# Attention and a channel mix on one core: from 448-token tiles, with receptance inside the attention stage, to 512-token tiles, with receptance by seven products in a stage of its own

## The chip, the cores and the metric

The kernel runs on one core of a Trainium2 chip. Its engines are TensorE (PE in the profile, with its weight loads as PEld), VectorE (DVE), ScalarE (ACT), GpSimd (POOL) and SyncE (SP); here SP issues every DMA, POOL does next to nothing. The metric is the time of one execution on the device in microseconds, the median of three runs.

## The reference, cut to what matters

```python
# q, k, v: 8 batches, 12 heads, 448 tokens, head size 64, float32
scores = scale * (q @ k.T) - log(448)
attn   = sigmoid(scores) @ v
x      = attn, heads joined                      # (8, 448, 768)
x_prev = x shifted by one token, zero in front
xk = mu_k * x + (1 - mu_k) * x_prev
xr = mu_r * x + (1 - mu_r) * x_prev
k  = relu(xk @ w_k)                              # w_k: 768 x 1024, float64
v  = (k * k) @ w_v                               # w_v: 1024 x 768, float64
out = sigmoid(xr @ w_r) * v                      # w_r: 768 x 768, float64
```

The three weights arrive as float64 and are turned into float32 by bit operations on DVE. Most products are made in three passes of a reduced format (fp32r): both operands are split into a high part (a cast on ACT or DVE) and a low part (a subtraction on DVE), and high x high, high x low and low x high are summed in a PSUM bank.

## The kernel before

**Order.** `Plan` (lines 23 to 95) takes operations with an engine, an estimated cost, a priority and the keys that they read and write; it plays them through by these costs and sends them out in that order. The order on each engine in the built program is the one that counts.

**Attention** (lines 306 to 403). 96 heads make 48 head pairs n. `prepare` splits q and k of a pair; `scores` makes three chunks of 128 keys (each 3 x 2 half-height matmuls into one of three double banks `sc`), `sigmoid` (ACT) turns a chunk into `pf`; `score_tails` and a sigmoid do the last 64 keys of two pairs at once; `weigh` and `weigh_tails` multiply with v in native fp32 into the banks `av`. `gather` copies the result to `xx`, stores x to `x_d`, mixes xr and splits it into `xr`, which stays in SBUF.

**Receptance** (lines 406 to 441) is a plain product: 48 units (8 batches x 6 blocks of 128 outputs), each 6 x 3 products of 448 columns. 40 units stand inside attention, from head pair 10 (`R_FROM`) on, between the score chunks, as 36 half-height matmuls each (L416); 8 follow it (L434 to L436). The whole of w_r stays in SBUF for this.

**Channel mix** (lines 541 to 732). Two stages: 0 is xk @ w_k, 1 is k2 @ w_v. Both use Strassen's scheme in Winograd's form: a pair of batches, that is two tiles of 448 tokens, and the halves of the weight give seven products instead of eight. Each product is a step of 36 matmuls (L664) into four banks `xb` or `yb`. The seven combined weights are made during attention (`convert_seven`), stored, and loaded and split into seven `slots` by `load_weight`. `fetch` loads x from `x_d` and mixes xk on ACT and DVE (L575, L576); `minus` forms the combinations of the data, `operand` splits them (L588, L589); `evacuate` adds the products up on DVE from PSUM and the copy `p1s` (L693 to L713), and `out_block` applies relu and square, or multiplies with the receptance `r_d`. There are 4 pairs x 7 = 28 steps in each stage. The products are put in the order 0, 1, 5, 4, 6, 2, 3.

Of the kernel before, what the change touches and what calls it, by code (L numbers as in the profile page):

```python
# [98 lines left out]
def attention_then_channel_mix(  # L99
# [33 lines left out]
    NEG_LOG_S = -math.log(S)  # L133

# [17 lines left out]

    WP, PFB, PTB, LEAD, RAW = 512, 9, 2, 2, 4
    WR_PACE, W_PACE = 0.9, 0.9
    R_FROM = 10
    CAST_DVE = "qk"
    LATE = 2

# [22 lines left out]
    wr_slots = ring(wp, "slot", 3, [P, 2 * WO], F32R)  # L181
    wr_at = [wr_slots[t // 4][:, t % 4 * DM:(t % 4 + 1) * DM] for t in range(2 * NJ)]
    wr_hi, wr_lo = wr_at[0::2], wr_at[1::2]
    gap(rpool, "gap0", 64)
    xr = ring(rpool, "xr", NJ, [P, 2, 2 * S], F32R)
    ro = ring(rpool, "ro", 2, [P, S], F32)
    wraw = ring(cpool, "wraw", 2, [P, WP, 2], U32)
    wbits = ring(cpool, "wbits", 8, [P, WP], U32)
    wexpo = ring(cpool, "wexpo", 1, [P, WP], U32)
# [13 lines left out]
    t1 = ring(apool, "t1", 2, [P, S], F32)  # L203
# [51 lines left out]
    def convert_wr(j, nh, at):  # L255
        src = w_r[j * P:(j + 1) * P, :].bitcast(U32)[:, 2 * nh * HN:2 * (nh + 1) * HN]
        u, U = spare(HN)
        w = convert(count[0], src, u, U, at)
        count[0] += 1
        hi, lo = (a[j][:, nh * HN:(nh + 1) * HN] for a in (wr_hi, wr_lo))  # L260
        key = ("wr", j, nh)
        op(ACT, act(HN, True), at, lambda: nc.scalar.copy(hi, w), [U], [key])
        op(DVE, dve(HN), at, lambda: nc.vector.tensor_sub(lo, w, hi), [U, key], [(key, "lo")])


    def convert_seven(w, out7, t, half_rows, n, pace, at):
# [506 lines left out]
```

## Time and profile before

| | us |
|---|---|
| runs | 845.71, 845.85, 844.97; median 845.71 |
| span of the profiled execution | 844.1 |
| PE busy | 829.9 |
| DVE busy | 625.8 |
| ACT busy | 465.0 |
| memory traffic | 157.73 MB, mean 187 GB/s |

The span goes from the first to the last instruction of the profiled execution; the profile gives no time of that execution beside it, so that what lies around the span is taken as the distance to the median of the runs, 1.6 us. Matmuls are pipelined: a record's duration (some 362 ns) is longer than the distance to the next one (some 200 ns), so a busy PE says only that it never ran dry; how fast it goes is read from the distance between starts.

### The profile page before, as it was taken

How to read it: one execution, taken by the hardware profiler on the slowest of the kernel's cores; microseconds unless marked ns; L12 is line 12 of the kernel's file. 1: busy time of each engine (PE TensorE's matmuls, PEld its weight loads, DVE VectorE, ACT ScalarE, POOL GpSimd, SP SyncE). 2: the span in 40 equal slices, each digit the busy share in tenths (PEclk: the TensorE clock that was granted, in tenths of full speed). 3: DMA queues.
4: the chain of work that ended last, by engine and by line, in shares of the span. 5: the costliest groups of instructions: out<-in, count | busy, mean ns of one | idle time of the engine just before them, and what ended most of it. 6: DMA issues, size and time to landing. Idle time of an engine off the chain costs nothing.

```text
span 844.1 us, 14681 instructions
## 1 busy us (share of the span) xinstructions
PE 829.9 (98%) x5424; PEld 669.4 (79%) x5424; DVE 625.8 (74%) x1169; ACT 465.0 (55%) x784; POOL 0.5 (0%) x8
## 2 busy tenths in 40 slices
PE   7999999999999999999999999999999999999997
PEld 4446766776667766776889999999999999999997
DVE  5999999999644343542579987969789795876955
ACT  5897556766566565664468384664746323233330
POOL 0000000000000000000000000000000000000000
PEclk9999999999999999999999999999999999999999
DMA  7777989888444433421677553443754557473415
GB/s 241 251 252 257 310 297 298 281 290 284 167 135 159 134 121 110 152 100 56 203 246 243 186 164 99 157 127 122 227 173 157 199 172 240 143 241 121 142 54 163
DMA packets 90934, 157.73 MB, mean 187 GB/s; under 512 B 10352, under 2 KB 79472, under 8 KB 90864
## 3 DMA queue, kind: packets, MB, share of 16 engines
q1 hardware_dynamic: 90864, 156.81, 56.6%
q8 instruction: 42, 0.69, 0.3%
q14 instruction: 28, 0.23, 0.1%
HBM read 98.05 MB, written 58.72 MB: 186 GB/s over the span
## 4 chain that ended last, share of the span: by engine, by line
PE 91%; DMA 3%; DVE 3%; ACT 2%; issue 1%; SPq 0%; POOLq 0%; DVEq 0%; POOL 0%; ACTq 0%
PE xb L664 26%; PE yb L664 20%; PE sc L416 17%; PE av L373 12%; PE sc L344 10%; PE sc L353 2%; PE av L382 2%; DMA x<-x_d 2%; DMA wraw<-in_moe_w_r 1%; DMA qn<-in_q 1%; DVE ys L576 0%; SPq L229 0%; ACT qh L222 0%; ACT ys L575 0%; DVE wbits L244 0%
## 5 line engine op out<-in xcount | busy, mean ns | idle before, releaser
L416 PE MATMUL sc<-xr,slot 64*128 64x448 f32 x1440 | 152.2, 361 | 1.0 <-ACT pf L365 1.0
L416 PEld LDWEIGHTS sc<-xr,slot 64*128 64x128 f32 x1440 | 133.3, 184 | 13.7 <-ACT pf L365 4.7
L365 ACT ACTIVATE pf<-sc 128x896 f32<-128x896 f32 x144 | 126.4, 923 | 14.5 <-PE sc L344 13.5
L588 ACT CAST rr<-ys 128x448 fp32r<-128x448 f32 x135 | 73.8, 568 | 107.0 <-PE xb L664 41.6
L373 PE MATMUL av<-pf,vn 128*64 128x448 f32 x576 | 114.6, 544 | 0.0
L664 PE MATMUL xb<-rr,slotc 128*128 128x448 f32 x450 | 93.0, 362 | 0.6 <-ACT p1s L693 0.6
L664 PE MATMUL yb<-rr,slot 128*128 128x448 f32 x450 | 92.9, 362 | 0.0
L589 DVE TENSOR_TENSOR rr<-ys,rr 128x448 fp32r<-128x448 f32 x135 | 80.7, 620 | 15.8 <-ACT rr L588 15.6
L664 PEld LDWEIGHTS xb<-rr,slotc 128*128 128x128 f32 x450 | 84.3, 187 | 6.6 <-ACT p1s L693 1.0
L664 PEld LDWEIGHTS yb<-rr,slot 128*128 128x128 f32 x450 | 84.4, 187 | 5.6
L373 PEld LDWEIGHTS av<-pf,vn 128*64 128x64 f32 x576 | 38.8, 136 | 62.2 <-issue 59.9
L344 PE MATMUL sc<-qh,kh 64*128 64x448 f32 x288 | 57.3, 395 | 5.4 <-ACT qh L222 4.4
L421 DVE TENSOR_TENSOR ro<-sc,ro 128x448 f32<-128x448 f32 x40 | 24.9, 623 | 44.7 <-ACT ro L420 44.5
L344 PE MATMUL sc<-ql,kh 64*128 64x448 f32 x288 | 53.6, 369 | 0.5 <-DVE ql L317 0.5
L365 ACT ACTIVATE pt<-sc 128x896 f32<-128x896 f32 x24 | 22.1, 921 | 57.4 <-PE sc L353 57.3
L344 PE MATMUL sc<-qh,kl 64*128 64x448 f32 x288 | 53.4, 368 | 0.1
L420 ACT COPY ro<-sc 128x448 f32<-128x448 f32 x40 | 21.4, 535 | 57.3 <-issue 33.2
L394 DVE COPY xx<-av 128x448 f32<-128x448 f32 x38 | 22.0, 622 | 40.3 <-PE av L382 40.1
L344 PEld LDWEIGHTS sc<-qh,kh 64*128 64x128 f32 x288 | 27.7, 189 | 29.8 <-issue 12.7
L664 PE MATMUL xb<-rr,slotb 128*128 128x448 f32 x225 | 46.5, 362 | 1.3 <-issue 1.3
L317 DVE TENSOR_TENSOR kl<-kn,kh 128x384 fp32r<-128x384 f32 x48 | 26.6, 555 | 25.8 <-ACT kh L222 25.7
L576 DVE SCALAR_TENSOR_TENSOR ys<-x,muk,ys 128x448 f32<-128x448 f32 x48 | 32.2, 683 | 18.1 <-ACT ys L575 18.1
(93 smaller groups left out, 1348.7 us busy)
## 6 DMA issues: line engine op xcount, KB each, us to landing
k_d<-cc SPq DMA_DIRECT2D x64, 224.0 KB, 2.0
kn<-in_k SPq DMA_DIRECT2D x48, 224.0 KB, 4.5
qn<-in_q SPq DMA_DIRECT2D x48, 224.0 KB, 4.7
vn<-in_v SPq DMA_DIRECT2D x48, 224.0 KB, 4.1
x_d<-xx SPq DMA_DIRECT2D x48, 224.0 KB, 3.9
r_d<-ro SPq DMA_DIRECT2D x48, 224.0 KB, 2.7
x<-x_d SPq DMA_DIRECT2D x48, 224.0 KB, 2.6
rt<-r_d SPq DMA_DIRECT2D x48, 224.0 KB, 2.9
```

The costliest lines, as they stand in the source:

```text
L317: op(DVE, dve(w), at, lambda src=src, hi=hi, lo=lo: nc.vector.tensor_sub(lo[i], src, hi[i]), R + [(a + "h", i)], [(a + "l", i)])
L344: nc.tensor.matmul(sc[u][:, h, :S], kk[half[h], c * P:(c + 1) * P], qq[half[h], :], start=e == 0, stop=e == 2)
L365: op(ACT, act(2 * S), at, lambda: nc.scalar.activation(f, sc[u][:, :, :S], AF.Sigmoid, bias=NEG_LOG_S, scale=SCALE), R, [K])
L373: nc.tensor.matmul(av[n % 2][half[h], :S], vn[n % 5][:, h * NC + c, :], pf[i][:, h, :], start=c == 0, stop=False)
L394: op(DVE, dve(S), at, lambda: nc.vector.tensor_copy(x[:, 1:], av[n % 2][:, :S]), [("av", n % 2)], [X])
L416: nc.tensor.matmul(t[:, h, :S], w[j][half[h], rows], xr[j][half[h], a, x], start=(j, e) == (0, 0), stop=(j, e) == (NJ - 1, 2))
L420: op(ACT, act(S), at, lambda: nc.scalar.copy(ro[o], t[:, 1, :S]), tk, [("ro", o)])
L421: op(DVE, dve(S), at, lambda: nc.vector.tensor_add(ro[o], t[:, 0, :S], ro[o]), tk + [("ro", o)], [("ro", o)])
L576: op(DVE, dve(S, ptr=True), at, lambda: nc.vector.scalar_tensor_tensor(y, x[:, 1:], muk[:, j:j + 1], y, ALU.mult, ALU.add), [X, Y], [Y])
L588: op(ACT, act(S, True), at, lambda: nc.scalar.copy(r[:, 0], y), [Y], [R])
L589: op(DVE, dve(S), at, lambda: nc.vector.tensor_sub(r[:, 1], y, r[:, 0]), [Y, R], [R + ("lo",)])
L664: nc.tensor.matmul(bank[:, :S], a, b, start=first and t == 0 and e == 0, stop=t == n - 1 and e == 2, skip_group_check=True)
```

## The change

- Tokens are numbered through all batches, 8 x 448 = 7 x 512, and the products work on tiles of 512. Three pairs of tiles take seven products each; the odd tile takes four with the weights of the same slots: products 0 and 1 sum up to one half of its outputs, and 0, 6 and 3 to the other.
- Receptance becomes a stage of its own, between attention and the two others, with the same seven products. Its weights (`convert_seven` with `to_slot`) go straight into the slots during attention. Nothing of receptance is left in attention.
- `gather` stores both mixes, `xr_d` and `xk_d`, made of one difference: x_prev + mu (x - x_prev). `fetch` loads them ready; L575 and L576 are gone.
- Of w_k's three row blocks one is converted during attention, two during receptance; w_v's four during the K stage.
- The sums are left in PSUM: product 0 is copied from `xb` to `yb` by ACT, and products 5, 6 and 3 are added onto it by the matmuls (no `start`). For this the four `yb` banks are written once by a matmul each (`prime`). Copies of products 5 and 4 are made by ACT; two additions per pair are left on DVE.
- Head pair 0 is multiplied in native fp32, unsplit. Splitting casts alternate between ACT and DVE by head pair. Some buffers of the next stage (`PRE` = 4 operands) lie outside the memory of attention.

Receptance's products, per pair of tiles 7 x 3 x 3 x 3 = 189 matmuls, per odd tile 4 x 27 = 108. In all 25 steps of 27, 25 of 36 and 25 of 36 matmuls of 512 columns.

```diff
+    T = 512
+    NT = B * S // T
+    R_, K_, V_ = range(3)
+    KT = (NJH, NJH, NFH)
+    CW = (DM // 2, DF // 2, DM // 2)
-    R_FROM = 10
-    CAST_DVE = "qk"
+    WR_FROM, WR_PACE, WK_EARLY = 1.0, 3.0, 1
+    PRE = 4
+    CAST_DVE = lambda n, a: n % 2 == 1
+    NATIVE = (0,)
...
+    def to_slot(t, n):
+        def put(p, a, at):
+            g = POS[p]
+            hi, lo = (slots[g][:, half * KT[R_] * n + t * n:half * KT[R_] * n + (t + 1) * n] for half in range(2))
+            K = ("slot", g, t)
+            op(ACT, act(n, True), at, lambda: nc.scalar.copy(hi, a[0]), [a[1]], [K])
+            op(DVE, dve(n), at, lambda: nc.vector.tensor_sub(lo, a[0], hi), [a[1], K], [K + ("lo",)])
...
     def gather(n, at):
...
+        op(ACT, act(S), at, lambda: nc.scalar.copy(x[:, 1:], av[n % 2][:, :S]), [("av", n % 2)], [X])
+        op(DVE, dve(S), at, lambda: nc.vector.tensor_sub(d, x[:, 1:], x[:, :S]), [X], [G])
+        for name, m, mu, to in (("mr", mr[n % 2], mur, xr_d), ("mk", mk[n % 2], muk, xk_d)):
+            M = (name, n % 2)
+            op(DVE, dve(S, ptr=True), at, lambda m=m, mu=mu: nc.vector.scalar_tensor_tensor(m, d, mu[:, j:j + 1], x[:, :S], ALU.mult, ALU.add), [X, G, (mu is muk, "mu")], [M])
+            dma(to[j][:, cols], m, at, [M], [])
...
-    def receptance_halves(b, i, at, u):
-    def receptance(b, i, at, bank):
...
+    PAIRS = [(2 * s, 2 * s + 1) for s in range(NT // 2)] + [(NT - 1,)]
...
     def right(stage, s, p, at):
+        if len(PAIRS[s]) == 1 and p in (6, 3):
+            used[stage, s, p] = used[stage, s, {6: 0, 3: 1}[p]]
+            return
...
+    def prime(i, at):
+        r, R = used[R_, 0, 0][0]
+        op(PE, mm(1, T), at, lambda: nc.tensor.matmul(yb[i], slots[0][:, :P], r[:, 0], start=True, stop=True, skip_group_check=True), [R] + slot_keys(0), [("yb", i)])
...
-                    nc.tensor.matmul(bank[:, :S], a, b, start=first and t == 0 and e == 0, stop=t == n - 1 and e == 2, skip_group_check=True)
+                    nc.tensor.matmul(bank, a, b, start=p in (0, 4) and (t, e) == (0, 0), stop=(t, e) == (n - 1, 2), skip_group_check=True)
...
     def evacuate(stage, s, p, i, at):
...
         if p == 0:
-            op(ACT, act(S), at, lambda: nc.scalar.copy(p1s[i], x), [X], [P1])
+            op(ACT, act(T), at, lambda: nc.scalar.copy(y, x), [X], [Y])
+        elif p == 5:
+            op(ACT, act(T), at, lambda: nc.scalar.copy(u2[i], y), [Y], [U])
+        elif p == 4:
+            op(ACT, act(T), at, lambda: nc.scalar.copy(p4[i], x), [X], [F])
...
+        elif p == 3:
+            finish(stage, s, 1, 0, i, y, [Y], None, at)
...
+    steps = [(stage, s, p) for stage in (R_, K_, V_) for s, pair in enumerate(PAIRS) for p in (ORDER if len(pair) == 2 else ODD)]
```

Where the built program's order moves, in three places. Numbers in the names are buffers.

PE in the middle of attention, before: the last product of a chunk of scores (L344), a receptance unit from the xr tiles and the w_r slots (L416), the next chunk, and the first products with v (L373).

```order
L344 MATMUL sc_296<-ql_272,kh_275 128x448 x2
L416 MATMUL sc_297<-xr_237,slot_233 128x448 x6
L416 MATMUL sc_297<-xr_238,slot_233 128x448 x6
L416 MATMUL sc_297<-xr_239,slot_234 128x448 x6
L416 MATMUL sc_297<-xr_240,slot_234 128x448 x6
L416 MATMUL sc_297<-xr_241,slot_235 128x448 x6
L416 MATMUL sc_297<-xr_242,slot_235 128x448 x6
L344 MATMUL sc_295<-qh_270,kh_275 128x448 x2
```

The same engine after, from the last chunk of scores (L341) of an odd head pair on: three products with v (L369), the next head pair's scores.

```order
L341 MATMUL sc_184<-ql_159,kh_162 128x448 x2
L369 MATMUL av_187<-pf_166,vn_146 64x448 x2
L369 MATMUL av_187<-pf_167,vn_146 64x448 x2
L369 MATMUL av_187<-pf_168,vn_146 64x448 x2
L341 MATMUL sc_185<-qh_156,kh_161 128x448 x2
```

The units of 36 matmuls between the chunks are gone, and the scores and the products with v follow each other directly.

DVE in attention, after, around a gather: the differences (L388) and the mixes (L391), the odd head pair's casts (L216) and low parts (L317), and pieces of the weight conversion (L236 to L238) in the gaps.

```order
L388 TENSOR_TENSOR dx_179<-xx_177 128x448
L236 TENSOR_SCALAR wexpo_141<-wraw_133 128x384
L391 SCALAR_TENSOR_TENSOR mr_182<-dx_179,mur,xx_177 128x448
L391 SCALAR_TENSOR_TENSOR mk_180<-dx_179,muk,xx_177 128x448
L216 CAST kh_162<-kn_143 128x384
L388 TENSOR_TENSOR dx_179<-xx_178 128x448
L317 TENSOR_TENSOR kl_164<-kn_143,kh_162 128x384
L391 SCALAR_TENSOR_TENSOR mr_183<-dx_179,mur,xx_178 128x448
L391 SCALAR_TENSOR_TENSOR mk_181<-dx_179,muk,xx_178 128x448
L216 CAST qh_157<-qn_153 128x448
L237 SCALAR_TENSOR_TENSOR wbits_136<-wraw_133,wbits_136 128x384
L317 TENSOR_TENSOR ql_159<-qn_153,qh_157 128x448
```

Before, at a like place, the copy out of `av` (L394) and the old mix (L399, L400) stood there, and the splits of xr (L403):

```order
L394 COPY xx_291<-av_298 128x448
L394 COPY xx_292<-av_299 128x448
L399 TENSOR_SCALAR t_293<-xx_291,omr 128x448
L399 TENSOR_SCALAR t_294<-xx_292,omr 128x448
L400 SCALAR_TENSOR_TENSOR t_293<-xx_291,mur,t_293 128x448
L400 SCALAR_TENSOR_TENSOR t_294<-xx_292,mur,t_294 128x448
L276 TENSOR_TENSOR wbits_250<-wbits_248,wbits_249 128x384
L241 TENSOR_SCALAR wbits_251<-wraw_245 128x384
L403 TENSOR_TENSOR xr_241<-t_293,xr_241 128x448
```

Per gather two mixes take the place of one, and the copy out of `av` has gone to ACT.

ACT at the end of attention, after: the last copies out of `av` (L387), the casts of step 1's operands (L472 into rrb), the copies of product 0 from `xb` to `yb` (L594). The casts of step 0 stand far ahead of this, in attention.

```order
L387 COPY xx_177<-av_187 128x448
L387 COPY xx_178<-av_188 128x448
L472 CAST rrb_2527<-ysb_2494 128x512
L594 COPY yb_2485<-xb_2487 128x512
L472 CAST rrb_2528<-ysb_2495 128x512
L594 COPY yb_2486<-xb_2488 128x512
L472 CAST rrb_2532<-ys_129 128x512
L594 COPY yb_2483<-xb_2489 128x512
```

Before, the first copies of product 0 (L693) came after receptance's last units, behind casts of the operands (L588) and weights (L459):

```order
L588 CAST rrb_4692<-ys_4412 128x448
L693 COPY p1s_4693<-xb_4678 128x448
L693 COPY p1s_4694<-xb_4679 128x448
L459 CAST slot_233<-wop_222 128x768
L588 CAST rr_4409<-ys_4418 128x448
```

Each copy of product 0 now stands between two casts whose data are fetched only after attention.

More of the change, by code (lines that the diff above doesn't have):

```diff
@@ L179, in attention_then_channel_mix @@
     pscore = psc.enter_context(tc.tile_pool(name="pscore", bufs=1, space=PSUM, side="right"))
[L181 to L189, printed above, removed]
+    slots = ring(base, "slot", 7, [P, 2 * WO], F32R)
+    gap(base, "gap0", 64)
+    rr = ring(base, "rr", PRE, [P, 2, T], F32R)
+    ys = ring(base, "ys", PRE, [P, T], F32)
+    wraw = ring(base, "wraw", 2, [P, WP, 2], U32)
+    wbits = ring(base, "wbits", 6, [P, WP], U32)
+    wexpo = ring(base, "wexpo", 1, [P, WP], U32)
     kn = ring(apool, "kn", RAW, [P, S], F32)
@@ L253, in spare, with convert_seven @@
         return wbits[i][:, :n], ("wbits", i)
[L255 to L266, printed above, removed]
+    def convert_seven(w, t, half_rows, n, pace, at, put):
         def get(rows_half, cols_half, at):
@@ L490, in key_chunks @@
             sigmoid(n, c, u, at + 0.1 * c)
-            if c in between and units:
-                receptance_halves(*units.pop(0), at + 0.1 * c, turn())
     def last_keys(n, at):
@@ L615, in right @@
                 operand(stage, s, p, 2, t, at)
[L617 to L628 removed]
     with tc.manual_schedule():
         plan.emit()
+    att.close()
@@ L648, in attention_then_channel_mix, with load_weight @@
+    wop = ring(vp, "wop", 2, [P, WO // 2], F32)
+    gap(vp, "gap4", 64)
+    rr += ring(vp, "rrb", 6, [P, 2, T], F32R)
     plan = Plan()
     op = plan.op
+    ncc, nrt, nw = [0], [0], [0]
+    def load_weight(stage, p, at):
+        g, src = POS[p], {K_: wk_o, V_: wv_o}[stage][p]
+        n = WO // 2
+        for h in range(2):
+            u = nw[0] % len(wop)
+            nw[0] += 1
+            w, W = wop[u], ("wop", u)
+            dma(w, src[:, h * n:(h + 1) * n], at, [("wo", id({K_: wk_o, V_: wv_o}[stage]), p, t) for t in range(NFH)], [W])
+            hi, lo = (slots[g][:, a * WO + h * n:a * WO + (h + 1) * n] for a in range(2))
+            K = ("slot", g, h)
+            op(ACT, act(n, True), at, lambda hi=hi, w=w: nc.scalar.copy(hi, w), [W], [K])
+            op(DVE, dve(n), at, lambda hi=hi, lo=lo, w=w: nc.vector.tensor_sub(lo, w, hi), [W, K], [K + ("lo",)])
@@ new lines, in attention_then_channel_mix @@
+    PREP, EVAC = -1.2, 0.3
+    steps = [(stage, s, p) for stage in (R_, K_, V_) for s, pair in enumerate(PAIRS) for p in (ORDER if len(pair) == 2 else ODD)]
+    first = {stage: next(i for i, x in enumerate(steps) if x[0] == stage) for stage in (R_, K_, V_)}
+    last = {(stage, p): max(i for i, x in enumerate(steps) if x[0] == stage and x[2] == p) for stage in (R_, K_, V_) for p in range(7)}
+    for stage, w, out7, pace in ((K_, w_k, wk_o, WK_PACE), (V_, w_v, wv_o, WV_PACE)):
+        at = first[stage - 1]
+        for t in range(WK_EARLY * (stage == K_), KT[stage]):
+            convert_seven(w, t, KT[stage], CW[stage], pace, at, to_dram(out7, t, CW[stage]))
+            at += 4 * pace
@@ L731, in attention_then_channel_mix @@
+    for at, (stage, s, p) in enumerate(steps):
+        right(stage, s, p, at + PREP)
+        rows = NFH if stage == K_ else NJH
+        if at == 0:
+            for i in range(4):
+                prime(i, 0.9)
+        for i in range(rows):
+            multiply(stage, s, p, i, at + i / rows)
+            evacuate(stage, s, p, i, at + i / rows + EVAC)
+        if stage < V_ and last[stage, p] == at:
+            load_weight(stage + 1, p, max(at + 1.5, first[stage + 1] - 8 + POS[p]))
     with tc.manual_schedule():
```

395 lines of the change are left out of this document (127 added, 268 removed).

## The prediction

> **What bounds the kernel now.** First the page's totals, the slices and the chain that ended last; of the four rows by slice, each digit is a tenth.
>
> ```profile
> PE 829.9 (98%) x5424; PEld 669.4 (79%) x5424; DVE 625.8 (74%) x1169; ACT 465.0 (55%) x784; POOL 0.5 (0%) x8
> ...
> PE   7999999999999999999999999999999999999997
> ...
> DVE  5999999999644343542579987969789795876955
> ...
> PEclk9999999999999999999999999999999999999999
> ...
> PE 91%; DMA 3%; DVE 3%; ACT 2%; issue 1%; SPq 0%; POOLq 0%; DVEq 0%; POOL 0%; ACTq 0%
> ```
>
> TensorE is the bound from end to end, at an undiminished clock. So the time is products times period, plus the places where PE stands. The chain in order of time gives the period, and the list of PE instructions the borders of the stages:
>
> ```profile
> 75.29 3.60 PE sc L416 x36
> ...
> 450.92 7.20 PE yb L664 x36
> ```
> ```profile
> 404.08 0.98 PE L382 MATMUL av<-pt,vn 64*64 64x448 f32 x8
> 405.00 0.47 PE L434 MATMUL sc<-xr,slot 128*128 128x448 f32 x1
> ...
> 435.35 7.45 PE L664 MATMUL xb<-rr,slotb 128*128 128x448 f32 x36 [1.26 <-issue]
> ...
> 832.35 7.36 PE L664 MATMUL yb<-rr,slot 128*128 128x448 f32 x36
> ```
>
> 7.20 us for 36 is 200.0 ns a matmul, and a receptance unit (18 pairs of half-height matmuls) is 3.60 us. Adding up: attention ends at about 404.9 us, with 40 units inside it (144.0 us), so 260.9 us are attention itself. Then 8 units (28.8) and 1.65 us of waiting to 435.35, 56 steps of 7.20 us (403.2) and 1.15 us of waiting to 839.7, and a tail of 4.4 us: 844.1 in all. The median of the runs, 845.71, stands 1.6 us above this span.
>
> **Term 1: how many products, and how long at 512 columns.** Before, 48 receptance units of 18 and 56 steps of 36: 864 + 2016 = 2880 matmuls' worth, 576.0 us. After, three pairs of tiles with 7 products and an odd tile with 4 make 25 steps in each of three stages: 25 x 27 + 25 x 36 + 25 x 36 = 2475. The question is their period. If it goes with the columns it is 200 x 512/448 = 228.6 ns and the 2475 take 565.7 us: hardly a gain. So what are the 200 ns made of?
>
> ```profile
> 6.10 0.58 PE L344 MATMUL sc<-qh,kl 64*128 64x448 f32 x2
> 6.48 0.58 PE L344 MATMUL sc<-ql,kh 64*128 64x448 f32 x2
> ```
> ```profile
> 28.96 2.48 PE L373 MATMUL av<-pf,vn 128*64 128x448 f32 x12
> ...
> 83.64 4.73 PE L373 MATMUL av<-pf,vn 128*64 128x448 f32 x24
> ```
> ```profile
> L664 PEld LDWEIGHTS xb<-rr,slotc 128*128 128x128 f32 x450 | 84.3, 187 | 6.6 <-ACT p1s L693 1.0
> ...
> L373 PEld LDWEIGHTS av<-pf,vn 128*64 128x64 f32 x576 | 38.8, 136 | 62.2 <-issue 59.9
> ```
>
> Three facts. The load of 128 columns takes 187 ns; only 13 ns of each period lie outside it. The native products load 64 columns in 136 ns, and twelve more of them cost (4.73 - 2.48)/12 = 187.5 ns each, below 200 at the same 448 columns. And at half clock, before PE warms up, the split products run every 374 ns (6.10 to 6.48), which is 2 x 187 and not 2 x 200. So streaming 448 columns takes about 187 ns, and 200 is a floor that the weight load sets. 512 columns stream for 187.5 x 512/448 = 214.3 ns, over the floor. I take 215 (the reading error of the subtraction allows 214.8): 2475 x 215 = **532.1 us**, against 576.0: 43.9 us less. Bounds: 214.3, and the proportional 228.6. Between lies a fixed 12.5 ns, 226.8.
>
> The Trainium skill, in "TensorE: Matmul & The Clock Gate", section "LDWEIGHTS (loading the stationary operand)", has a load take P/1.2 ns, 107 ns for 128 columns; by that the load would hide under any product here, the 13 ns would belong to the matmul, and the 226.8 would hold. The trace's 187 ns row disagrees with it, so the row decides. The same page's gap N/2.4 + 2.5, section "Back-to-back issue gap", would give 215.8 at 512 and 2 us more than my sum; at 448 it gives 189, and the trace has 200.
>
> **Term 2: attention without receptance in it.** On PE, the 260.9 us stay, if PE is fed. Where the kernel before runs attention alone (its first ten head pairs) a pair of head pairs takes this long on PE:
>
> ```profile
> 22.53 0.47 PE L344 MATMUL sc<-qh,kh 64*128 64x448 f32 x2
> ...
> 33.03 0.47 PE L344 MATMUL sc<-qh,kh 64*128 64x448 f32 x2
> ...
> 54.86 0.47 PE L344 MATMUL sc<-qh,kh 64*128 64x448 f32 x2
> ...
> 66.60 0.47 PE L344 MATMUL sc<-qh,kh 64*128 64x448 f32 x2
> ```
>
> 10.50 us where nothing waits, 11.74 in the worst. 22.5 + 22 x 10.5 + 7.5 for the last = 261.0, the same figure. But until now 3.6 us units filled PE while DVE caught up; afterwards nothing does. DVE's work per pair comes from these rows:
>
> ```profile
> L317 DVE TENSOR_TENSOR ql<-qn,qh 128x448 fp32r<-128x448 f32 x48 | 29.7, 620 | 0.1
> L317 DVE TENSOR_TENSOR kl<-kn,kh 128x384 fp32r<-128x384 f32 x48 | 26.6, 555 | 25.8 <-ACT kh L222 25.7
> L400 DVE SCALAR_TENSOR_TENSOR t<-xx,mur,t 128x448 f32<-128x448 f32 x48 | 31.0, 680 | 0.0
> L222 DVE CAST qh<-qn 128x448 fp32r<-128x448 f32 x7 | 2.7, 387 | 0.2 <-DMA qn<-in_q 0.2
> L222 DVE CAST kh<-kn 128x384 fp32r<-128x384 f32 x7 | 2.5, 357 | 3.8 <-DMA kn<-in_k 3.3 <-PE sc L344 0.5
> ...
> L245 DVE SCALAR_TENSOR_TENSOR wbits<-wexpo,wbits 128x384 f32<-128x384 uint32 x28 | 15.5, 554 | 0.3
> L242 DVE TENSOR_SCALAR wexpo<-wraw 128x384 uint32<-128x384 uint32 x28 | 10.0, 357 | 0.0
> L276 DVE TENSOR_TENSOR wbits<-wbits,wbits 128x512 f32<-128x512 f32 x12 | 8.1, 685 | 0.0
> L242 DVE TENSOR_SCALAR wexpo<-wraw 128x512 uint32<-128x512 uint32 x12 | 5.1, 422 | 0.0
> ```
>
> Two pairs of splits 2.35, the odd head pair's casts 0.74, two gathers of a subtraction (0.62) and two mixes (0.68) 3.96: 7.05 us, 127 for 18 such pairs. Beside them come w_r (12 pieces of 3 x 0.554 + 2 x 0.357, 12 combinations and 21 low halves of 0.555: 47 us) and the first third of w_k at 512 columns (4 pieces of 3 x 0.685 + 2 x 0.422 and 4 combinations, and a piece begun: 17), and three first operands (2): 193 us, where PE needs 18 x 10.5 = 189. So DVE, not PE, paces the first three quarters of this stage. It kept up like this:
>
> ```profile
> 25.00:50.00 25.00, 24.71 (x178) 11.96 (x174) 24.79 (x58) 23.18 (x38) 0.00 (x0) 1.00 0.85 279
> 50.00:75.00 25.00, 22.71 (x172) 12.39 (x172) 23.27 (x50) 24.02 (x42) 0.00 (x0) 1.00 0.74 244
> ```
>
> (Columns: length, then PE, PEld, DVE, ACT busy.) DVE was 99% and 93% busy. At 97%, from 25.4 us where the first pair's gather can start, the other 182 us end 188 us later, at 213. PE unhindered ends pair 18 at 21.7 + 17 x 10.5 = 200; DVE's gather ends 4 us after that when nothing is late, and the splits that stand beside it are read another 4 us later. So PE loses what exceeds 208, 5 to 6 us; I take **6**; 0 at the least, 22 if each of 18 pairs takes 11.74. ACT is no bound:
>
> ```profile
> L365 ACT ACTIVATE pf<-sc 128x896 f32<-128x896 f32 x144 | 126.4, 923 | 14.5 <-PE sc L344 13.5
> ...
> L222 ACT CAST qh<-qn 128x448 fp32r<-128x448 f32 x41 | 23.7, 577 | 0.1
> ```
>
> 7 sigmoids of 0.923, two casts and two copies of some 0.55 each and one w_r cast make 9.2 us a pair. Head pair 0 unsplit saves two casts at the start but takes four passes for three; I count 1 us less. Attention then ends at 265.9 us.
>
> **Term 3: from attention into receptance.** Before, this border cost 1.65 + 1.15 us. After, the four priming matmuls take 0.9 us and wait for the two last ACT copies of av, 1.3 us after the last product (two copies, 0.53 each in a row below, and the handover). Step 0 has its operands, split during attention. Step 1 has one of three: the other buffers lie where attention's lie, so their fetch (a single SP queue) stands behind the last four mix stores, which wait for six DVE operations (3.97 us), and behind their landing.
>
> ```profile
> k_d<-cc SPq DMA_DIRECT2D x64, 224.0 KB, 2.0
> ...
> x<-x_d SPq DMA_DIRECT2D x48, 224.0 KB, 2.6
> ```
>
> Counted from the last product of attention: the first copy ends at 0.8 us, the six operations at 4.8, the store has landed at 7.0, the fetch (2.6) at 9.6, its cast ends at 10.2, and the copy that frees step 1's bank, queued behind this cast on ACT, at 10.8. PE is through step 0 (27 x 0.215) at 8.0 and waits 2.8 us. Then step 2's third operand stands behind nine DVE operations that take their turn only then, three of a w_k piece among them: some 2.4 us more. 1.3 + 2.8 + 2.4 = 6.5; bounds 1.3 (the fetch early enough) and 10 (a store at three times its price). With the priming 7.4.
>
> **What is hidden.** The p0 copy into a bank is an ACT write to PSUM, which no row shows; nearest are the copy out of a bank and the cast between SBUF tiles.
>
> ```profile
> L693 ACT COPY p1s<-xb 128x448 f32<-128x448 f32 x28 | 14.8, 531 | 15.1 <-PE xb L664 15.0
> L588 ACT CAST rr<-ys 128x448 fp32r<-128x448 f32 x135 | 73.8, 568 | 107.0 <-PE xb L664 41.6
> ```
>
> 0.53 to 0.65 us at 512 columns. It must end before the next product's same row, two or three rows of 1.9 us later; that cover is good for 3.9 us. Per seven receptance steps (40.6 us) DVE has 39 operations of 0.69, 27 us, and with 30 us of w_k and 13 of slots some 128 of 145 us; ACT some 26 of 41. The other stages are longer for the same work. I count 1.15 us of small waits as before. **Tail:** the last block is multiplied straight from its bank, one DVE operation fewer:
>
> ```profile
> 839.75 0.62 DVE L713 TENSOR_TENSOR cc<-yb,p1s 128x448 f32<-128x448 f32 x1 [1.11 <-PE yb L664]
> 840.41 0.63 DVE L684 TENSOR_TENSOR cc<-cc,rt 128x448 f32<-128x448 f32 x1
> ```
>
> 4.4 - 0.6 = 3.8.
>
> **Sum.** 265.9 + 7.4 + 532.1 + 1.15 + 3.8 = 810.4 us of span; with the 1.6 us, **812 us**, 4.0% less.
>
> **The rivals.** (a) The 12.5 ns are a fixed part of each matmul: 2475 x 11.8 = 29 us more, 841. The 374 ns at half clock and the 187.5 speak against it. (b) The change gains nothing: a product costs what its columns cost, 228.6 ns, 33.7 us more, 846: same. (c) Attention runs at its worst observed pace, 11.74 us: 16 more, 828. For it: ACT and DVE were both near full there, and DVE will be again; against: ACT has less to do. (d) Slower: the seeded banks chain each step to an ACT copy that stands in line behind casts waiting for DVE. One late ACT operation (0.62 us) in each of 75 steps is 46 us, 858; it decides from (845.7 - 812)/75 = 0.45 us a step. Against it: the same bank was freed by the same engine before, and over all steps PE waited once:
>
> ```profile
> PE xb L664 <- ACT p1s L693: 0.6, 1, 0.6
> ```
>
> **How the numbers follow.** Forecast 0.70; (c) 0.11; (a) 0.08; (b) 0.04; (d) 0.07. The forecast's own span is 803 (no DVE loss, 214.3 ns, little lost at the border) to 822 (DVE loss doubled, border 10). To leave out no more than (a), (b), (d) the range reaches over (c): 803 to 831. Under 0.2% a measurement of this kernel can't tell from no change; faster 0.89 ((a) too), same 0.04, slower 0.07.
>
> **What would show it.** The period within a step: 215 ns or 227. The pair period in attention: 10.5, and DVE over 95% busy in it. Attention's end at 266, the first K step near 419, the V stage near 613. Wrong would be: PE waits for ACT at step starts all along, or a period near 228.

## The result, and the profile after

| | before | after |
|---|---|---|
| median of the runs, us | 845.34 (844.64 to 845.85, 4 runs) | 853.05 (852.84 to 853.69, 4 runs) |
| span of the profiled execution, us | 844.1 | 851.1 |
| matmuls recorded | 5424 | 4297 |
| memory traffic, MB | 157.73 | 179.63 |

The ratio is 1.0094, with a 95% interval of 1.0080 to 1.0109: the change makes the kernel **0.9% slower**, where 4.0% faster (812 us, 803 to 831) was forecast.

The experiments came in three sets on three chips, each with runs of the kernel before beside them: e1 to e4 (its median there 845.16 us), e5 to e8 (845.25) and e9 and e10 (844.09). Ratios below are to the kernel before of the same set; differences of some 1 us between sets mean little.

The page of the kernel after, its totals, three of the rows by slice, and the chain that ended last:

```profile
PE 831.4 (98%) x4297; PEld 593.5 (70%) x4297; DVE 583.5 (69%) x1040; ACT 476.3 (56%) x773; POOL 0.3 (0%) x6
...
PE   8998999998999899999999999999999999999998
...
DVE  4878888886765698988887973725835486594621
...
PEclk9998999998999999999999999999999999999999
...
PE 93%; DMA 3%; DVE 2%; issue 1%; ACT 1%; SPq 0%; DVEq 0%; ACTq 0%
```

PE is still busy from end to end, so the time went either into longer products or into the few places where PE stood. Between its two ends its row falls in slices 4, 10 and 14, and in the first two of them the granted clock falls too; before, neither did. Slice 14 (276.6 to 297.9 us) holds the border of the stages. First the products. The chain in order of time, in the K stage:

```profile
451.11 8.19 PE yb L556 x36
459.30 8.32 PE xb L556 x36
...
484.07 8.16 PE yb L556 x36
```

8.16 to 8.32 us for 36 products is 226.7 to 231 ns each, not 215. Next the waits of PE, grouped (engine, line, releaser: us in total, times, longest):

```profile
PE sc L341 <- ACT pt L362: 5.6, 2, 3.1
PE sc L341 <- DMA qn<-in_q: 4.1, 1, 4.1
PE xb L556 <- ACT yb L594: 3.1, 1, 3.1
PE sc L341 <- ACT pf L362: 2.0, 1, 2.0
PE yb L543 <- ACT xx L387: 1.1, 1, 1.1
```

The wait for `qn` is the start of the program and the ones for `yb` and `xx` are the border. New are the two rows in which attention's scores wait for a sigmoid. The list of PE instructions, at the first score products of three pairs of head pairs and at all that show a wait:

```profile
51.00 0.47 PE L341 MATMUL sc<-qh,kh 64*128 64x448 f32 x2
...
61.54 0.47 PE L341 MATMUL sc<-qh,kh 64*128 64x448 f32 x2
...
64.40 0.47 PE L341 MATMUL sc<-qh,kh 64*128 64x448 f32 x2 [1.98 <-ACT pf L362]
...
67.86 0.74 PE L341 MATMUL sc<-qh,kh 64*128 64x448 f32 x2 [2.58 <-ACT pt L362]
...
79.09 0.47 PE L341 MATMUL sc<-qh,kh 64*128 64x448 f32 x2
...
194.87 0.47 PE L341 MATMUL sc<-qh,kh 64*128 64x448 f32 x2
...
199.42 0.74 PE L341 MATMUL sc<-qh,kh 64*128 64x448 f32 x2 [3.07 <-ACT pt L362]
...
211.42 0.47 PE L341 MATMUL sc<-qh,kh 64*128 64x448 f32 x2
```

A pair of head pairs takes 10.54 us (51.00 to 61.54), as forecast, but two of them take 17.55 and 16.55: 13.0 us more in all. What ACT did in the first of them:

```profile
56.44 1.73 ACT L362 ACTIVATE pf<-sc 128x896 f32<-128x896 f32 x2 [1.82 <-PE sc L341]
62.91 0.62 ACT L472 CAST rr<-ys 128x512 fp32r<-128x512 f32 x1 [4.75 <-DMA ys<-xr_d]
63.44 0.91 ACT L362 ACTIVATE pf<-sc 128x896 f32<-128x896 f32 x1
```

And SP's queue at the same time:

```profile
53.15 0.38 SPq L223 DMA_DIRECT2D xr_d<-mr  x1
...
57.45 0.32 SPq L223 DMA_DIRECT2D xk_d<-mk  x1
59.72 2.38 SPq L223 DMA_DIRECT2D ys<-xr_d  x2
62.19 0.86 SPq L223 DMA_DIRECT2D vn<-in_v  x2
```

ACT stands 4.75 us in front of a cast, with the next sigmoid right behind it. The cast (L472) belongs to receptance's first step, which begins some 210 us later. Its operand is fetched from the mix `xr_d`, which had only just been stored (issued at 53.15). SP issues the fetch only at 59.72, when that store has landed, with the next heads' loads behind it. Then ACT waits for the fetch. The second place is alike on ACT, with the fourth such operand. Here SP issued the fetch at 192.63 without waiting for a store, and it took 4.8 us to land:

```profile
197.50 0.62 ACT L472 CAST rr<-ys 128x512 fp32r<-128x512 f32 x1 [2.70 <-DMA ys<-xr_d]
198.02 0.53 ACT L387 COPY xx<-av 128x448 f32<-128x448 f32 x1
198.44 0.92 ACT L362 ACTIVATE pt<-sc 128x896 f32<-128x896 f32 x1
```

Part of each loss isn't waiting at all. Three stretches of the kernel after (columns: length, busy PE, PEld, DVE, ACT, POOL, granted clock, DMA share, GB/s):

```profile
65.20:72.00 6.80, 4.22 (x16) 1.83 (x16) 6.80 (x15) 5.46 (x9) 0.00 (x0) 0.50 0.68 218
198.30:205.10 6.80, 5.68 (x18) 2.07 (x18) 5.42 (x12) 3.56 (x5) 0.00 (x0) 0.50 0.79 281
283.60:287.00 3.40, 3.40 (x9) 2.62 (x9) 2.63 (x5) 1.87 (x5) 0.00 (x0) 0.50 0.97 349
```

Behind each stall of 2 to 3 us in this run TensorE runs at half its clock, 6.8 us in attention and 3.4 at the border. Last, the border from attention into receptance, from the list of PE instructions:

```profile
270.86 0.98 PE L377 MATMUL av<-pt,vn 64*64 64x448 f32 x8
272.94 1.20 PE L543 MATMUL yb<-rr,slot 128*128 128x512 f32 x4 [1.10 <-ACT xx L387]
273.98 6.35 PE L556 MATMUL xb<-rr,slot 128*128 128x512 f32 x27
283.38 1.48 PE L556 MATMUL xb<-rr,slot 128*128 128x512 f32 x3 [3.05 <-ACT yb L594]
```

### The profile page after: what moved, and what is told of

It is laid out like the page before. It is cut to its first block, busy times and chain, and to the rows that moved or that the text cites. A ratio compares the mean times of both kernels' runs of the same rounds, so it can differ in the third digit from the quotient of the medians.

```text
span 851.1 us, 12546 instructions
## 1 busy us (share of the span) xinstructions
PE 831.4 (98%) x4297; PEld 593.5 (70%) x4297; DVE 583.5 (69%) x1040; ACT 476.3 (56%) x773; POOL 0.3 (0%) x6
## 2 busy tenths in 40 slices
DMA packets 98128, 179.63 MB, mean 211 GB/s; under 512 B 11152, under 2 KB 45456, under 8 KB 98064
## 4 chain that ended last, share of the span: by engine, by line
PE 93%; DMA 3%; DVE 2%; issue 1%; ACT 1%; SPq 0%; DVEq 0%; ACTq 0%
PE xb L556 37%; PE yb L556 29%; PE av L369 12%; PE sc L341 11%; PE av L377 2%; PE sc L350 2%; DMA ys<-xr_d 1%; DMA xr_d<-mr 1%; DVE mr L391 0%; DVE mk L391 0%; DMA qn<-in_q 0%; DMA xk_d<-mk 0%; ACT xx L387 0%; DMA ysb<-xr_d 0%; ACT pt L362 0%
## 5 line engine op out<-in xcount | busy, mean ns | idle before, releaser
L556 PE MATMUL xb<-rrb,slot 128*128 128x512 f32 x816 | 198.4, 393 | 0.0
L556 PEld LDWEIGHTS xb<-rrb,slot 128*128 128x128 f32 x816 | 154.0, 189 | 33.8
L556 PE MATMUL yb<-rrb,slot 128*128 128x512 f32 x696 | 169.5, 391 | 0.0
L556 PEld LDWEIGHTS yb<-rrb,slot 128*128 128x128 f32 x696 | 130.6, 188 | 28.8
L556 PE MATMUL xb<-rr,slot 128*128 128x512 f32 x570 | 142.1, 394 | 3.2 <-ACT yb L594 3.1
L556 PEld LDWEIGHTS xb<-rr,slot 128*128 128x128 f32 x570 | 107.2, 188 | 28.2 <-ACT yb L594 3.5
L473 DVE TENSOR_TENSOR rrb<-ysb,rrb 128x512 fp32r<-128x512 f32 x106 | 70.6, 688 | 75.0 <-ACT rrb L472 74.9
L369 PE MATMUL av<-pf,vn 128*64 128x448 f32 x576 | 122.0, 560 | 0.0
L556 PE MATMUL yb<-rr,slot 128*128 128x512 f32 x393 | 100.0, 393 | 0.0
L472 ACT CAST rrb<-ysb 128x512 fp32r<-128x512 f32 x106 | 63.3, 619 | 34.7 <-PE xb L556 12.4
L369 PEld LDWEIGHTS av<-pf,vn 128*64 128x64 f32 x576 | 38.0, 139 | 61.9 <-issue 56.4
L341 PE MATMUL sc<-qh,kh 64*128 64x448 f32 x282 | 57.7, 405 | 7.6 <-ACT pt L362 5.6
L341 PEld LDWEIGHTS sc<-qh,kh 64*128 64x128 f32 x282 | 26.5, 185 | 45.7 <-ACT xx L387 15.5
L341 PE MATMUL sc<-ql,kh 64*128 64x448 f32 x282 | 52.0, 365 | 0.0
L341 PE MATMUL sc<-qh,kl 64*128 64x448 f32 x282 | 51.6, 363 | 0.0
L594 ACT COPY yb<-xb 128x512 f32<-128x512 f32 x40 | 22.8, 571 | 46.0 <-PE xb L556 46.0
L317 DVE TENSOR_TENSOR kl<-kn,kh 128x384 fp32r<-128x384 f32 x47 | 26.1, 555 | 29.0 <-ACT kh L216 28.9
L473 DVE TENSOR_TENSOR rr<-ysb,rr 128x512 fp32r<-128x512 f32 x46 | 30.6, 687 | 19.8 <-ACT rr L472 19.6
L388 DVE TENSOR_TENSOR dx<-xx 128x448 f32<-128x448 f32 x48 | 29.9, 622 | 20.8 <-ACT xx L387 20.3
L472 ACT CAST rr<-ysb 128x512 fp32r<-128x512 f32 x46 | 28.0, 621 | 24.9 <-DVE cc L586 11.2
```

The costliest lines, as they stand in the source:

```text
L317: op(DVE, dve(w), at, lambda src=src, hi=hi, lo=lo: nc.vector.tensor_sub(lo[i], src, hi[i]), R + [(a + "h", i)], [(a + "l", i)])
L341: nc.tensor.matmul(sc[u][:, h, :S], kk[half[h], c * P:(c + 1) * P], qq[half[h], :], start=e == 0, stop=e == len(pairs) - 1)
L369: nc.tensor.matmul(av[n % 2][half[h], :S], vn[n % 5][:, h * NC + c, :], pf[i][:, h, :], start=c == 0, stop=False)
L388: op(DVE, dve(S), at, lambda: nc.vector.tensor_sub(d, x[:, 1:], x[:, :S]), [X], [G])
L472: op(ACT, act(T, True), at, lambda: nc.scalar.copy(r[:, 0], y), [Y], [R])
L473: op(DVE, dve(T), at, lambda: nc.vector.tensor_sub(r[:, 1], y, r[:, 0]), [Y, R], [R + ("lo",)])
```

## The experiments

**1. What the period of a product is made of (e1).** Rows of 12 to 60 matmuls of one shape, one behind another while ACT and DVE do next to nothing, in the split format (fp32r), in native fp32 and in bf16, with weights of 128, 96, 64 and 32 columns. Its core:

```python
def run(kind, M, N, count):
    t, bank = kinds[kind], banks[nb[0] % 8]
    nb[0] += 1
    for i in range(count):
        w = t[:, 512 + i % 4 * 128:512 + i % 4 * 128 + M]
        nc.tensor.matmul(bank[:M, :N], w, t[:, :N], start=i == 0, stop=i == count - 1)
```

> This kernel computes nothing of the reference: it runs streams of 40 matmuls of one shape after each other, with nothing else on the chip, to read the distance between starts. Columns theory (the split format streams at 0.4465 ns a column whatever else runs): 228.6 ns at 512 columns, 214 at 480, 200 at 448, 186 at 416, 171 at 384, the same with weights of 96, 64 and 32 columns. Fixed-part theory (streaming at 0.4185 ns a column plus 12.5 ns): 226.8, 213.4, 200, 186.6, 173.2. Weight-load theory (my prediction's): 215 at 512 and 200 from 480 down to 128, and with weights of 64 and 32 columns 215 and 187. Interference theory (other engines and transfers slow the streams in the kernel): 215 at 512 and 189 or less at 448 here. Power theory (the data's switching slows the array): zero operands come out at 215 and 188, random ones at 229 and 200. Native fp32 and 16-bit streams give the unburdened rate for comparison.

Distances between starts, the mean over the last half of a row, and the length of the weight-load records:

```
split, 128 weight columns:  512 -> 226.7   480 -> 216.7   448 -> 202.7   416 -> 186.7
                            384 -> 173.3   320 -> 146.7   256 -> 120.0   128 -> 111.7 ns
split, 96 / 64 / 32:        512 -> 230.0 / 230.2 / 231.7   448 -> 202.7 / 202.1 / 202.3
all operands zero:          512 -> 226.7   448 -> 202.7
native fp32, per record:    512 -> 429.2   448 -> 375.8
bf16:                       512 -> 215.8   448 -> 189.2
weight load, split:         128 columns 188, 96: 161, 64: 134, 32: 108; bf16, 128: 98
```

The groups of its PE instructions by form give the same to a reader (columns: busy us, mean ns of one record; a row of 40 back to back has 39 distances and one record):

```profile
L47 PE MATMUL bank<-zero 128*128 128x512 f32 x40 | 9.3, 390 | 0.0
...
L47 PE MATMUL bank<-split 128*128 128x384 f32 x40 | 7.1, 335 | 0.0
...
L47 PE MATMUL bank<-split 128*128 128x256 f32 x40 | 5.0, 283 | 0.0
```

(7.1 - 0.335)/39 = 173 ns and (5.0 - 0.283)/39 = 121. From 256 to 512 columns the period grows by 106.7 ns, 0.4167 a column, and 13.3 ns are left over at either end: 120.0 - 106.7 and 226.7 - 213.3. So a split product costs **13.3 ns plus 0.4167 ns a column**. A weight load of 188 ns is no floor, since at 256 columns the products start 120 ns apart, and loads of 108 ns at 32 columns don't shorten the period either. Data don't matter: all zeros take the same. Work on ACT and DVE isn't the cause either, since they were idle. Proportion falls too: from 226.7 it would give 113.3 at 256.

The law isn't exact everywhere. At 448 and 480 columns the rows lie 2.7 and 3.4 ns above it; experiment 5 finds the reason for 448. At 128 columns the products come every 111.7 ns where it gives 66.7, so some other bound sets in there; no product of the two kernels is that narrow.

**2. The early fetches held back (e2).** One element is written into each of the four early operands' buffers from a later mix, so that the planner can place fetch and cast only then. Nothing of the result changes, and the first four operands are still ready before attention ends.

```diff
+    HOLD = {24 + 4 * i + 2 * (t is rr): (i, t) for i in range(PRE) for t in (ys, rr)}
...
+            if name == "mr" and n in HOLD:
+                i, t = HOLD[n]
+                op(DVE, 60, at, lambda m=m: nc.vector.tensor_copy(t[i][:, :1] if t is ys else t[i][:, 0, :1], m[:, :1]), [M], [(t is ys, i)])
```

> The changed kernel, but the fetches and splits of the first four receptance operands are held back: one-element copies on DVE, after the gathers of head pairs 24 to 38, write into their buffers first, so that a fetch comes long after the stores it reads, and a cast long after its fetch. Early-fetch theory (these fetches wait on the SP queue for a store to land, loads of q, k, v stand behind them, and the casts that wait for them stand in front of the sigmoids on ACT): the two pairs of 17.6 and 16.5 us fall back to 10.5, 13 us less, the half clock in attention goes: 840 us. Rival (attention alone is at the limit of DVE and ACT): stalls of the same sum come at other places, 850 to 853.

840.07 us (839.57 to 841.2), ratio to before 0.9933 (0.9906 to 0.9959). The waits of PE in it:

```profile
PE sc L341 <- DMA qn<-in_q: 4.1, 1, 4.1
PE xb L561 <- ACT yb L599: 3.0, 1, 3.0
PE yb L548 <- ACT xx L389: 1.1, 1, 1.1
```

Both waits for sigmoids are gone, and nothing took their place: 13.0 us less, the 13.0 that the two long pairs had cost.

**3. One at a time (e6, e7).** The same edit for the first three operands only, and for the fourth only.

```diff
-    HOLD = {... for i in range(PRE) for t in (ys, rr)}
+    HOLD = {... for i in range(PRE) for t in (ys, rr) if i < 3}      # e6
+    HOLD = {... for i in range(PRE - 1, PRE) for t in (ys, rr)}      # e7
```

> Only the first three of the four early operands are held back; the fourth's fetch stays where it was. Early-fetch theory: the 17.6 us pair goes, the 16.5 us pair stays: 7.1 us off 853, 846. Rival, that the stalls come from a common shortage (bandwidth, or ACT as a whole) that merely shows at these places: another pair stalls in its stead, 850 or more.

> Only the fourth operand is held back. Early-fetch theory: the 16.5 us pair goes, the 17.6 us pair stays: 6.0 us off 853, 847. Rival, a common shortage: 850 or more.

e7 gave 847.18 us (846.14 to 848.89), as expected. e6 gave 842.2 (841.34 to 843.89), 4 us less than expected. In its profile the fourth operand's stall is there, but short, in the list of PE instructions:

```profile
199.40 0.47 PE L341 MATMUL sc<-qh,kh 64*128 64x448 f32 x2
...
206.01 0.47 PE L341 MATMUL sc<-qh,kh 64*128 64x448 f32 x2 [1.28 <-ACT pf L362]
...
211.70 0.47 PE L341 MATMUL sc<-qh,kh 64*128 64x448 f32 x2
```

That pair takes 12.30 us, and the granted clock stays full. With the first stall gone the rest of attention runs earlier, and the same fetch happens to cost PE 1.28 us in place of 3.07. So the first stall belongs to the first three operands and the second to the fourth, and no other pair stalls instead. But the price of the fourth isn't fixed: 1.8 or 6.0 us. What decides it, how the fetch falls among the other transfers perhaps, is not shown.

**4. The width alone (e3, e4).** The kernel after with tiles of 448 tokens (eight tiles, four pairs, no odd one), with the early fetches as they are and held back.

```diff
-    T = 512
+    T = 448
...
-    PAIRS = [(2 * s, 2 * s + 1) for s in range(NT // 2)] + [(NT - 1,)]
+    PAIRS = [(2 * s, 2 * s + 1) for s in range(NT // 2)] + [(NT - 1,)] * (NT % 2)
```

> The changed kernel with tiles of 448 tokens: eight tiles, four pairs of seven products, no odd tile, 28 steps of 27, 36 and 36 matmuls: 2772 instead of 2475. Columns theory: 2772 x 0.200 = 554 us against 567, 12 us less: 841, if the early fetch costs the same. Weight-load theory with some other burden on the changed kernel's steps: the products keep 229 ns, or the saving is lost to the larger number of operand and evacuation operations: 853 or more.

> Both edits: 853 - 13 - 12 = 828 us, below the kernel before (845). If the two are not independent, or either theory is wrong, 840 or more.

The two runs, e3 and e4, gave 842.96 us (840.78 to 844.77), ratio 0.9974 (0.9959 to 0.9989); and 833.61 (832.2 to 834.91), ratio 0.9854 (0.9826 to 0.9882). So the wider tile gains nothing, it costs: 6.5 us with the fetches held back (840.07 against 833.61) and 10.1 without (853.05 against 842.96; holding them is worth 13.0 us at 512 and 9.4 at 448). By experiment 1's law 2475 products of 226.7 ns are 561.0 us and 2772 of 200.0 are 554.4, 6.6 us less: the four pairs stream fewer columns, 2772 x 448 = 1.242 million against 2475 x 512 = 1.267, since the odd tile's four products save nothing, and the fixed part for 297 products more, 4.0 us, doesn't outweigh that. e4 came out 5.6 us above its expectation, and the chain shows why: its steps of 36 take 7.20 to 7.31 us. On the mean of all distances between starts a product takes 201.9 ns and not 200.0, just as 512 columns take 229.5 in the kernel after and not 226.7. So this comparison isn't of the width alone yet; experiment 6 gives a cleaner one.

In e3 two pairs stall as well, by 4.3 and 3.2 us. The second of them shows that the length of a stall doesn't decide about the clock: PE stands for 2.94 us, nearly the 3.07 of the kernel after, and runs on at full clock (the second line's columns are those of the stretches above).

```profile
196.43 0.47 PE L341 MATMUL sc<-qh,kh 64*128 64x448 f32 x2 [2.94 <-ACT pt L362]
```
```profile
196.40:200.00 3.60, 3.58 (x22) 1.60 (x24) 2.96 (x7) 2.39 (x3) 0.00 (x0) 1.00 0.84 287
```

**5. The last 2 ns (e5).** Rows of matmuls with the moving data or the weights shifted in SBUF, and in the kernel's own pattern; two more rows were meant to run beside a busy ACT and DVE.

```python
for sh in (0, 16, 32, 48, 64, 96):        # columns of 4 bytes
    run(N, lambda i: sh, lambda i: i % 4 * 128)          # moving data shifted
for sh in (16, 32, 64, 96):
    run(N, lambda i: 0, lambda i: sh + i % 4 * 128)      # weights shifted
```

> The kernel computes nothing of the reference: rows of matmuls in the split format, 128 x 128 weights, 512 and 448 columns, with the moving data or the weights shifted by 64 to 384 bytes, in the kernel's own pattern of high, low, high, and, in one group for each width, while ScalarE and VectorE copy and subtract. It asks where the 2.5 ns above 226.7 (after: 229.3 on the mean) and the 1.9 above 200.0 come from. Placement: some shifts give 226.7 and 200.0, others 228 to 231 and 202 to 203, the same with the other engines idle. Interference: all shifts give 226.7, and only the groups beside busy engines give 229. The pattern of high and low parts: only those groups give 229.

```
moving data shifted by, bytes:
            0       64      128     192     256     384
512    226.7    229.0    232.4    233.3    226.7    233.3 ns
448    202.7    200.0    204.0    202.3    206.7    204.0 ns
weights shifted instead:  512: 64 -> 233.3, 128 -> 232.4, 256 -> 226.7, 384 -> 232.4 ns
kernel's pattern of high and low parts, shifted by 0 / 64:  512: 226.7 / 229.0;  448: 202.7 / 200.0
```

Placement moves the period by as much as is looked for, the pattern of high and low parts adds nothing, and the best place depends on the width: 64 bytes for 448 columns, 0 or 256 for 512. The distance between data and weights isn't the whole of it: at 448 columns, 256 bytes on the data give 206.7, and 256 on the weights 202.7.

Interference was not tested as planned. The copies and subtractions ran at the start of the program:

```profile
4.85 18.26 ACT L61 COPY a<-a 128x512 f32<-128x512 f32 x28 [2.84 <-DVE a L58]
```
```profile
10.34 20.31 DVE L62 TENSOR_TENSOR d<-d,raw 128x512 f32<-128x512 f32 x28
```

The rows meant to run beside them came at 332.7 and 343.6 us, alone. By chance the first two rows, both of 512 columns at shift 0, did run beside them: the first, up to 21.4 us, beside both engines, the second mostly beside DVE alone. Both took 226.7 all the same (the first over its last half). For 448 columns no row here tests it; experiment 6 does, in the kernel.

The kernel before has all its split operands 64 bytes past a multiple of 256 from the weight slots, by its paddings, and runs at 200.0. The kernel after keeps the padding of 64 for its first four operands, where 512 columns want 0, and has the other six at 0. With 448 columns in this layout the four lie well and the six don't. The trace of the kernel after bears this out, but not in size: its 12 steps with all operands at 64 take 229.2 ns a product, the 29 with all at 0 take 227.6, and the 34 that mix both take 231.2, more than either place alone. Why mixing costs more stays open.

**6. The placement mended in both (e9, e10).** In e2's kernel the padding before the first ring goes from 64 to 256 bytes; in e4's the padding beside the second ring moves.

```diff
-    gap(base, "gap0", 64)
+    gap(base, "gap0", 256)                                # e9, T = 512: all at 0
...
-    gap(vp, "gap4", 64)
     rr += ring(vp, "rrb", 6, [P, 2, T], F32R)
+    gap(vp, "gap4", 192)                                  # e10, T = 448: all at 64
```

> The kernel of e2_hold (512 tokens, early fetches held back, 840.1) with one padding changed from 64 to 256 bytes, so that every split operand lies at a distance from the weight slots that is a multiple of 256 bytes; the order on every engine stays. Placement theory: 226.7 ns a matmul for 229.3, 2475 x 2.7 = 6.6 us less, 833.5. Rival, that the 2.7 ns come from the other engines or from the row starts of a step: 229 stays, 840.

> The kernel of e4_t448_hold (448 tokens, fetches held back, 833.6) with the padding beside the second ring of split operands moved, so that all ten lie 64 bytes off the multiples of 256 (before, four lay at 64 and six at 0). Placement theory: 200.0 ns a matmul for 201.9, 2772 x 1.9 = 5.3 us less, 828.3. Rival: 201.9 stays, 833.6.

e9: 834.28 us (832.69 to 834.83), ratio 0.9876 (0.9857 to 0.9895). e10: **828.74 us** (828.24 to 829.4), ratio 0.9816 (0.9796 to 0.9836), the fastest of all. Steps of 36 in the chain of e9:

```profile
649.47 8.16 PE xb L561 x36
657.63 8.16 PE yb L561 x36
```

and of e10:

```profile
549.08 7.20 PE yb L561 x36
556.28 7.20 PE xb L561 x36
```

Now every step takes the same, 226.7 and 200.0 ns a product, mixed ones too and with ACT and DVE as busy as before. So other engines add nothing to be seen: one padding, and the surplus is gone. The gains, 5.8 and 4.9 us by the medians and 4.7 and 3.8 if the kernels before of the two sets are made equal, are somewhat below the 6.6 and 5.3 expected; PE's wait at the border grew by 0.5 and 0.4 us (3.01 to 3.48, 3.94 to 4.34).

e9 against e10 is also the cleanest comparison of the two widths, in one set, with fetches held and operands well placed: the wider tile costs 5.5 us, where experiment 1's law gives 6.6.

**7. More operands before the border (e8).** e4's kernel with six early operands in place of four, so that step 1 needs no fetch after attention; the ring of sigmoid outputs makes room.

```diff
-    WP, PFB, PTB, LEAD, RAW = 512, 9, 2, 2, 4
+    WP, PFB, PTB, LEAD, RAW = 512, 8, 2, 2, 4
-    PRE = 4
+    PRE = 6
-    HOLD = {24 + 4 * i + ...
+    HOLD = {22 + 4 * i + ...
```

> Tiles of 448 tokens, fetches held back, and six operands in place of four outside the memory of attention, so that steps 0 and 1 need no fetch after it; the ring of sigmoid outputs goes from 9 to 8 buffers to make room. Border theory: PE's wait of some 3 us before step 1 and the half clock behind it go, 4 to 5 us off 833.6, 829. Rival: the eighth buffer is missed in attention, or the wait moves to step 2, whose operands are fetched after attention still: 832 to 835.

833.44 us (832.87 to 833.83) against 833.61: nothing gained. The list of PE instructions shows the wait one step later:

```profile
262.14 10.96 PE L561 MATMUL xb<-rr,slot 128*128 128x448 f32 x54
275.29 0.44 PE L561 MATMUL yb<-rrb,slot 128*128 128x448 f32 x1 [2.19 <-issue]
276.25 2.61 PE L561 MATMUL yb<-rrb,slot 128*128 128x448 f32 x6 [0.52 <-DVE rrb L478]
```

Steps 0 and 1 (54 products) run through, and step 2 waits, by the second line for its own operands. The half clock behind it lasts 6.8 us, where it was 3.4 in e4. That is the rival's outcome. A fix would have to bring the fetches of at least three steps, not two, ahead of attention's end; this was not tried.

## Why the prediction was wrong

Its sum, against what the profile of the kernel after shows:

| term, us | forecast | measured | |
|---|---|---|---|
| attention ends | 265.9 | 271.7 | 270.86 + some 0.8 |
| border, with priming | 7.4 | 7.0 | 2.3 + 3.05 + some 1.7 of half clock |
| 2475 products | 532.1 | 568.4 | 847.2 (last product) - 273.98, less 3.05 and 1.7 |
| small waits | 1.15 | 0 | the list of waits has no others |
| tail | 3.8 | 3.9 | 851.1 - 847.2 |
| around the span | 1.6 | 2.0 | 853.05 - 851.1 |

**Term 1 was mis-sized by 36.3 us, and it is what turned the forecast.** The step that failed is "200 is a floor that the weight load sets. 512 columns stream for 187.5 x 512/448 = 214.3 ns, over the floor." That the streaming of 448 columns takes 187 ns was right: 448 x 0.4167 is 186.7. But the 13 ns that remain aren't a floor that wider products clear; they are added to a product of every width from 256 to 512 columns (experiment 1). 226.7 - 215 is 11.7 ns, times 2475 is 28.9 us: rival (a), which got a chance of 0.08. Another 7.4 us come from placement, 2475 x (229.5 - 226.7) = 6.9, and a small rest. No row of the trace before could show that cost, since there every operand lay right.

Two rows had spoken against (a), and neither did. The native products of attention, "(4.73 - 2.48)/12 = 187.5 ns each", are of another format: one behind another on their own they take 375.8 ns a record (experiment 1), so that 187.5 is a half of that, got where the products of two heads alternate between the halves of a bank, and it holds nothing of the split format's fixed part. The 374 ns at half clock are read rightly, but say nothing of full clock: the nine products of 512 columns in the stretch from 283.60 to 287.00 start some 427 ns apart, twice 213.3 without any fixed part. So the fixed part is there at full clock and not at half. One can't halve a period that was measured at half clock and call what is missing a floor. Why it vanishes there stays open.

On the weight load the Trainium skill had it right where the prediction overruled it. By "TensorE: Matmul & The Clock Gate", section "LDWEIGHTS (loading the stationary operand)", a load takes P/1.2 ns, 107 ns for 128 columns. A load of that length hides under any product here, and the 13 ns then belong to the product; the prediction set this aside because the load's record lasts 187 ns. By experiment 1 the record's length is no bound on the pace: beside loads with records of 188 ns, products start 120 ns apart at 256 columns, and 111.7 at 128. The gap of N/2.4 + 2.5 ns in the Trainium skill (same page, section "Back-to-back issue gap") agrees with bf16, 215.8 and 189.2 ns measured; for the split format the measured addition is 13.3.

**Term 2 was 5.8 us short, the sum of two larger errors.** DVE was to pace attention and cost 6 us. It did not. Between the stalls the period is the 10.5 us that PE needs, with DVE busy 87% of the time (95.45 of 110 us):

```profile
80.00:190.00 110.00, 110.00 (x796) 54.97 (x794) 95.45 (x196) 85.27 (x129) 0.00 (x0) 1.00 0.81 261
```

What was missed instead are the early fetches. The prediction counted "three first operands (2)" as DVE work in attention, and the order of the built program showed their casts far ahead. It did not follow the fetches and casts into the two queues in which they stand: SP's, where the first fetch waits for a store to land, and ACT's, where the next sigmoid stands behind the cast. They cost 13.0 us (experiments 2 and 3). Together: 265.9, less 6 for DVE, less 2 for a start 3 us earlier where 1 was counted, plus 13 and a remainder of 0.8, is 271.7.

**Term 3 was right in sum.** The waits forecast as 1.3 and 2.8 were 1.10 and 3.05; the third, 2.4, didn't come, and half a clock behind the second, not foreseen, took nearly as much. The fetch behind the last mix stores is what set it, as worked out: SP issues it only at 279.29, and ACT's cast in front of the copies of product 0 waits 9.34 us for it.

```profile
282.22 0.62 ACT L472 CAST rrb<-ysb 128x512 fp32r<-128x512 f32 x1 [9.34 <-DMA ysb<-xr_d]
```

Single prices were low: the mix stores land in 5.1 us (median of the 48) where 2.0 was taken from the K stage's stores; the page before had a nearer row, attention's own stores of x at 3.9. Experiment 7 moves this wait and doesn't remove it.

**The rivals.** (a), a fixed part of each product, is the mechanism that happened. (c), attention at 11.74 us a pair, has the size of the loss (16 against 13) but not the place: all other pairs run at 10.5. (d), the slower case, didn't happen: PE waits for the copy of product 0 once, 3.1 us at the border, not in 75 steps. The kernel became slower without it, by (a) and the early fetches together: 841 + 13 is 854, and 853.05 came. That this comes so near is luck: the 7.4 us of placement and rest are about made up by the 8 that DVE and the earlier start didn't cost. The list of what would show it named the period, and with "a period near 228" the way in which it was wrong.

What of the change is worth keeping is in e10: receptance by seven products, the seeded banks and fewer operations in attention, without the wider tile, with the fetches held and the operands placed right, are 15.35 us, 1.8%, better than the kernel before in the same set of runs (844.09).

## What to carry to other kernels

A period at one width is one equation for two unknowns: before scaling it to another width, measure a second width in the same number format, alone, and don't take the length of a load's record for a floor. When a planner brings work of a later stage forward, follow each instruction it issues, its DMAs and its casts too, to the queue in which it stands, and ask what it waits for and who stands behind it. A padding that was tuned for one tile width has to be tuned again for another.

## What the runs showed of the hardware that was not expected

- A well placed split (fp32r) product of 256 to 512 columns costs 13.3 ns beside its 0.4167 ns a column, bf16 some 2.5 (215.8 - 213.3); at half clock the split product shows no such part (426.7 at 512 columns, 374 at 448).
- Where moving data and weights lie in SBUF changes the period by some 3%: 226.7 to 233.3 ns at 512 columns, 200.0 to 206.7 at 448, with the best place at 0 or 256 bytes for the one and 64 for the other.
- Within attention and at its border, a stall of PE of 2 to 4.3 us was followed by 3.4 or 6.8 us at half clock in every case but one, and its length decides neither: 2.19 us in e8 (with 0.52 soon after) brought 6.8, 4.34 in e10 brought 3.4, and 2.94 in e3 none, like the 1.28 in e6. The clock changes on a grid: in the kernel after, the stretches at full clock between two falls last 126.29 and 78.51 us, 37 and 23 times 3.413. In e3 a point of this grid lies within the stall and leaves some 1.3 and 1.7 us of it on either side. That this is why the clock stayed full is likely, but not shown. In pairs of head pairs, the 3.07 us of the kernel after cost 6.0 us and the 2.94 of e3 cost 3.2.
